# Leaving out the products of zeros at the start of a four-layer transformer kernel

## The chip, the cores and the metric

The kernel runs on one core of one Trainium2 chip. A core has five engines, each working through its own list of instructions in order: TensorE (PE, with its weight loads shown apart as PEld), VectorE (DVE), ScalarE (ACT), GpSimd (POOL) and SyncE (SP), which here only issues DMAs. The metric is the time of one execution on the device in microseconds (us); lower is better.

## The reference

The input x is 2048 tokens of 576 numbers in bf16. Two kinds of layer alternate, A, B, A, B, each added to x after a normalisation of its input:

```python
x = x + A(layernorm(x)); x = x + B(layernorm(x))
x = x + A(layernorm(x)); x = x + B(layernorm(x))

# A: linear attention, 32 heads of 18
q, k, v = split(x @ wqkv)                       # 576 -> 3 * 576
pq = q @ w_phi[h]; pk = k @ w_phi[h]            # per head, 18x18
phi_q = concat(softmax(pq), softmax(-pq)); phi_k likewise
kv = phi_k^T @ v;  z = sum over tokens of phi_k
o = (phi_q @ kv) / (phi_q . z + 1e-6);  return o @ wo
# B: gated, without a nonlinearity
return ((x @ w_gate) * (x @ w_up)) @ w_down     # 576 -> 4608 -> 576
```

## The kernel before

**Stages.** The tokens are cut into 16 tiles of 128. The first microseconds prepare the A layers: `w_phi` and the q and k parts of `wqkv` (loaded as five blocks of rows into `Wraw`) are multiplied together once, so that one product per tile gives pq or pk. For each block this takes five transposes on PE (L1235), a copy out of PSUM (L1238), and products with a block-diagonal form of `w_phi` called `BDphi` (L1249). Then layer A runs over the tiles (projections at L1366, sums at L1608), then layer B in eight pairs of tiles (L1902 for gate and up, L1976 and L1978 for down), and both again for the second pair of layers.

**The flag.** The softmaxes can leave out the subtraction of the maximum when the weights are small enough. The kernel finds out on the chip. `t_flag` forms, for each of the five blocks of `Wraw`, ten products of a 128x128 piece with itself (L1109), summed over the blocks in two PSUM banks; VectorE takes the maxima (L1112), compares them with a bound made from `w_phi` (`t_m2`: L1088 on VectorE, L1091 and L1094 on PE, L1118 on VectorE), two tiny products (L1120) gather the outcome, and VectorE writes the flag (L1122). Every engine then loads the flag (L315) and branches (L316). What follows the branch exists twice, a fast and a general program; all work of the layers lies behind it. Here the fast one runs.

**The order of the work.** The program writes all engines' lists at build time. A planner (`Sched`) holds generators ("threads") that ask for operations, keeps a modelled time for each engine, and takes either the thread that a long list of names written out by hand (`ORDER`) says comes next or, when that list is used up, the one that can start first. A thread that needs a PSUM bank takes the free one whose last modelled use is the oldest (`_try_acquire`, `bank_time`).

**The products of zeros.** `t_init` first has VectorE set a 128x128 tile `zt` to zero (L1005), and then tells the planner that it has a filler (L1007). From there on, whenever the planner is about to place PE work, it calls `keep_warm` with the modelled start of that work. Where PE's modelled gap before it is over 350 ns (1000 ns behind the branch), filler products are put there, each a 128x128 piece of zeros with itself into a free PSUM bank that nothing reads (L1067):

```python
b = max(cand)[1]
cold = 2.0 if t < self.warm_at else 1.0
n = int((limit - (150.0 if early else 400.0) - t) / (56.0 * cold))
for _ in range(n):
    o = self.fill(b, self.pe_mode)
```

They end in the model before the work that they stand in front of. `limit` is the modelled start of that work, `t` is PE's modelled time, `cand` holds the free banks with the time of their last use. In the program that runs there are 25 of them, all ahead of PE's first other instruction.

Of the kernel before, what the change touches and what calls it, by code (L numbers as in the profile page):

```python
# [797 lines left out]
class K:  # L798
# [203 lines left out]
    def t_init(self):  # L1002
        s = self
        yield ("ops", "dve", [
            Op(80, lambda e: e.memset(s.zt[:], 0.0), writes=[("zt",)]),  # L1005
        ])
        s.sc.fill = s.filler  # L1007
        yield ("ops", "dve", [
            Op(100, lambda e: e.memset(s.epst[:], EPS), writes=[("epst",)]),
            Op(100, lambda e: e.memset(s.eps6[:], 1e-6), writes=[("eps6",)]),  # L1010
# [1256 lines left out]
```

## Time and profile before

| | |
|---|---|
| median of 4 runs | 1059.44 us (1058.93 to 1061.63) |
| profiled execution, its own time | 1061.01 us |
| its span, from first to last instruction | 1059.3 us |
| PE busy | 1051.6 us, 99% of the span, 15853 products |
| DVE, ACT, POOL busy | 480.0, 345.6, 193.5 us |
| chain of work that ended last | PE 96%, DMA 2%, DVE 1%, ACT 1% |
| products of zeros (L1067) | 25, from 1.04 us on, the last begun at 3.6 us |
| flag written (L1122) | 11.74 us |

The profile is of one execution. Its busy time of PE counts each product from its start to its modelled end, so neighbours overlap in it; the distance from one start to the next is what a product takes from PE's time. The granted clock is printed as 1.00 in every stretch, the first microseconds too. A releaser behind an idle time is inferred from semaphores. The 1.7 us between span and own time lie before the first and behind the last instruction.

### The profile page before, as it was taken

What the parts mean: (1) busy time and instruction counts of PE and PEld (TensorE: products, weight loads), DVE (VectorE), ACT (ScalarE), POOL (GpSimd) and SP (SyncE); (2) the same over time, 40 slices, a digit from 0 to 9 for tenths busy, and PEclk for the clock granted to TensorE, in tenths of its full rate; (3) what the DMA queues carried; (4) which work ended last, traced back from release to release, by engine and by line L of the source; (5) the groups of instructions that cost most, each with busy time, mean ns of one, the idle gap of its engine ahead of it and who ended that gap; (6) DMA issues with size and microseconds to landing.
All of it is one profiled execution on the core that took longest, in us unless ns stands there. A gap on an engine that the chain in (4) does not pass through costs nothing.

```text
span 1059.3 us, 34388 instructions
## 1 busy us (share of the span) xinstructions
PE 1051.6 (99%) x15853; PEld 804.6 (76%) x15853; DVE 480.0 (45%) x971; ACT 345.6 (33%) x836; POOL 193.5 (18%) x208
## 2 busy tenths in 40 slices
PE   9999999999999999999999999999999999999998
PEld 7778868687786868778696786878777786868684
DVE  7885544354544435444242753534344343424131
ACT  7775314143241414224141732222213131303020
POOL 4952112030222203013010120202010101000000
PEclk9999999999999999999999999999999999999999
DMA  5694281653608164342606035535372818080704
GB/s 172 109 357 134 44 232 38 185 79 92 159 22 229 28 196 68 105 125 42 205 7 202 4 57 166 108 116 135 91 172 57 206 23 239 15 226 15 213 2 149
DMA packets 177626, 127.79 MB, mean 121 GB/s; under 512 B 96576, under 2 KB 175680, under 8 KB 176320
## 3 DMA queue, kind: packets, MB, share of 16 engines
q1 hardware_dynamic: 176864, 125.47, 45.7%
q8 instruction: 126, 2.06, 0.8%
q14 instruction: 28, 0.23, 0.1%
q10 hardware_dynamic: 608, 0.02, 0.0%
HBM read 100.82 MB, written 2.36 MB: 97 GB/s over the span
## 4 chain that ended last, share of the span: by engine, by line
PE 96%; DMA 2%; DVE 1%; ACT 1%; issue 0%
PE ps L1902 54%; PE ps L1976 22%; PE ps L1366 13%; PE ps L1978 3%; PE ps L1760 1%; DMA wdr<-in_B_w_down_dram 1%; PE ps L1608 1%; DMA wdx<-in_B_w_down_dram 0%; PE ps L1354 0%; PE ps L1333 0%; DVE dd_h1g L1569 0%; DMA wst<-in_A_w_phi_dram 0%; PE ps L1249 0%; DVE ss_w4f L1554 0%; ACT dd_h1g L1487 0%; PE ps L1109 0%
## 5 line engine op out<-in xcount | busy, mean ns | idle before, releaser
L1902 PE MATMUL ps<-xT,Wu 64*128 64x256 bf16 x4608 | 581.5, 269 | 0.0
L1902 PE MATMUL ps<-xT,Wg 64*128 64x256 bf16 x4608 | 580.7, 269 | 0.1
L1902 PEld LDWEIGHTS ps<-xT,Wg 64*128 64x128 bf16 x4608 | 430.4, 94 | 31.2 <-issue 3.7
L1902 PEld LDWEIGHTS ps<-xT,Wu 64*128 64x128 bf16 x4608 | 431.6, 94 | 27.8
L1951 DVE TENSOR_TENSOR hT<-ps,hT 128x512 bf16<-128x512 f32 x288 | 199.1, 691 | 302.2 <-ACT hT L1949 302.1
L1949 ACT CAST hT<-ps 128x512 bf16<-128x512 f32 x288 | 168.4, 585 | 401.0 <-PE ps L1902 397.6
L1976 PE MATMUL ps<-wdr,hT 128*128 128x512 bf16 x960 | 245.5, 380 | 0.9 <-DMA wdr<-in_B_w_down_dram 0.8
L1569 POOL TENSOR_TENSOR dd<-dd,ss 128x576 bf16<-128x576 bf16 x92 | 107.1, 1190 | 440.0 <-ACT ss L1565 440.0
L1978 PE MATMUL ps<-wdr,hT 128*128 128x64 bf16 x960 | 184.9, 193 | 0.0
L1976 PEld LDWEIGHTS ps<-wdr,hT 128*128 128x128 bf16 x960 | 93.8, 98 | 112.3 <-DMA wdr<-in_B_w_down_dram 2.9
L1902 PE MATMUL ps<-xT,Wr 64*128 64x256 bf16 x1152 | 164.7, 269 | 0.0
L1322 POOL TENSOR_SCALAR xln<-x_sb,nmean,rstd 128x576 bf16<-128x576 bf16 x58 | 47.2, 822 | 324.9 <-DVE nmean L1303 142.5
L2019 DVE TENSOR_TENSOR x_sb<-ps,x_sb 128x64 bf16<-128x64 f32 x32 | 7.0, 220 | 211.5 <-PE ps L1978 211.5
L1978 PEld LDWEIGHTS ps<-wdr,hT 128*128 128x128 bf16 x960 | 94.1, 98 | 0.2
L1565 ACT ACTIVATE ss<-ss 128x64 f32<-128x64 f32 x92 | 23.8, 260 | 197.9 <-DVE ss L1554 196.9
L1554 DVE TENSOR_REDUCE ss<-dd 128x64 f32<-128x1152 bf16 x48 | 63.7, 1344 | 12.6 <-ACT dd L1487 8.9
L1902 PEld LDWEIGHTS ps<-xT,Wr 64*128 64x128 bf16 x1152 | 62.8, 94 | 6.5
L1976 PE MATMUL ps<-wdx,hT 128*128 128x512 bf16 x192 | 54.3, 380 | 0.2 <-DMA wdx<-in_B_w_down_dram 0.2
L1366 PE MATMUL ps<-Wv,xT 64*128 64x288 bf16 x576 | 49.2, 283 | 0.0
L1366 PE MATMUL ps<-Wk,xT 64*128 64x288 bf16 x576 | 48.0, 283 | 0.3 <-ACT dd_h1g L1487 0.2
L1289 DVE BATCH_NORM_STATS2 st<-x_sb 128x6 f32<-128x288 bf16 x120 | 46.2, 444 | 0.6 <-DMA x_sb<-in_A_x_dram 0.6
L1366 PE MATMUL ps<-Wq,xT 64*128 64x288 bf16 x576 | 41.2, 283 | 0.1
(129 smaller groups left out, 742.8 us busy)
## 6 DMA issues: line engine op xcount, KB each, us to landing
wdr<-in_B_w_down_dram SPq DMA_DIRECT2D x240, 288.0 KB, 3.7
wdx<-in_B_w_down_dram SPq DMA_DIRECT2D x48, 288.0 KB, 3.6
Wg<-in_B_w_gate_dram SPq DMA_DIRECT2D x4, 1152.0 KB, 17.2
Wu<-in_B_w_up_dram SPq DMA_DIRECT2D x4, 1152.0 KB, 18.8
out_dram<-x_sb SPq DMA_DIRECT2D x16, 144.0 KB, 2.4
x_sb<-in_A_x_dram SPq DMA_DIRECT2D x7, 288.0 KB, 3.8
Wraw<-in_A_wqkv_dram SPq DMA_DIRECT2D x5, 304.0 KB, 4.7
xT<-xln SPq DMA_TRANSPOSE x54, 2.5
```

Of the source, the lines that this page charges most:

```text
L1289: ops.append(Op(d_dve(288), (lambda e, j=j, h=h, src=src: e.bn_stats(st[:, sl[j], 6 * h:6 * h + 6], src)), reads=rd, writes=[("st", sl[j], ...
L1322: em = (lambda e, j=j: e.tensor_scalar(xln[:, sl[j], 0:576], x_sb[:, ss[j], :], s.nmean[:, sl[j]:sl[j] + 1], rstd[:, sl[j]:sl[j] + 1], ALU ...
L1366: out.append(Op(61, (lambda e, h=h, k=k, st=(i == 0 and k == 0), sp=(i == 1 and k == 3): e.matmul(s.ps[:, banks[h], 0:N], L[r, k, :], Wm[r ...
L1554: Op(1265, (lambda e: e.tensor_reduce(ss[:, sm, :], e4, AX.X, ALU.add)), reads=s.ddk(sm, 0) + s.ddk(sm, 1), writes=[("ss", sm)]),
L1565: yield ("ops", "act", [Op(200, (lambda e, kw=kw: e.activation(ss[:, sm, :], ss[:, sm, :], **kw)), reads=[("ss", sm)], writes=[("ss", sm)])])
L1569: yield ("alt", [(eng, [Op(dur, (lambda e, ev=ev, rb=rb: e.tensor_tensor(ev, ev, rb, ALU.mult)), reads=s.ddk(sm, br) + [("ss", sm)], write ...
L1608: ops.append(Op(d_pe(CW * n) + 3, (lambda e, k=k, c0=c0, h=h, n=n, st=(first and k == bi): e.matmul(s.ps[:, bank, c0:c0 + CW * n], phi[:, ...
L1902: out.append(Op(54.3, (lambda e, bank=bank, cs=cs, lhsT=lhsT, rhs=rhs, st=st, sp=sp: e.matmul(ps[:, bank, cs].rearrange("p (a n) -> p a n" ...
L1949: yield ("ops", "act", [Op(480, (lambda e, gb=gb, p=p: e.copy(hT[:, p, :], ps[:, gb, :])), reads=[("gu", gb)], writes=[("hT", p)] + (s.raw ...
L1951: yield ("ops", "dve", [Op(600, (lambda e, ub=ub, p=p: e.tensor_tensor(hT[:, p, :], ps[:, ub, :], hT[:, p, :], ALU.mult)), reads=[("gu", u ...
L1976: ops = [Op(d_pe(512), (lambda e: e.matmul(s.ps[:, bank, 0:512], lhsT, s.wslot(slot)[:, fi, 0:512], start=(f == 0), stop=(f == NF - 1))), ...
L1978: Op(d_pe(64) + 3, (lambda e: e.matmul(s.ps[:, z, 64 * sl:64 * sl + 64], lhsT, s.wslot(slot)[:, fi, 512:576], start=(f == 0 and (sl == 0 o ...
```

## The change

The planner is told that it has no filler. `keep_warm` is then never called, and the program has no instruction of L1067. The tile `zt` is still set to zero (L1005), though nothing reads it any more. Nothing else of the text of the kernel differs.

```diff
@@ t_init
             Op(80, lambda e: e.memset(s.zt[:], 0.0), writes=[("zt",)]),
         ])
-        s.sc.fill = s.filler
+        s.sc.fill = None
         yield ("ops", "dve", [
```

## The prediction

> **What bounds the kernel now.** I began with the page: the span and the chain of work that ended last.
>
> ```profile
> span 1059.3 us, 34388 instructions
> ...
> PE 96%; DMA 2%; DVE 1%; ACT 1%; issue 0%
> ```
>
> PE carries 96% of the chain, so what delays PE for good delays the end. But the change touches only the first 4 us, so the question is what bounds that stretch. The tile view of zt tells what goes:
>
> ```profile
> L1067 PE MATMUL ps<-zt x25: 289/314/314, 1.0 to 3.6; 128*128 128x128 bf16 x25
> ```
>
> Then the timeline of PE (start, length, engine, line, operation, operands, count):
>
> ```profile
> 1.04 2.85 PE L1067 MATMUL ps<-zt 128*128 128x128 bf16 x25 [1.04 <-DVE eps L1010]
> 3.87 1.24 PE L1109 MATMUL ps<-Wraw 128*128 128x128 bf16 x10
> 4.91 0.47 PE L1235 MATMUL ps<-ident,Wraw 128*128 128x128 bf16 x5
> 5.22 0.72 PE L1109 MATMUL ps<-Wraw 128*128 128x128 bf16 x10
> 6.09 0.38 PE L1091 MATMUL ps<-identf,cst 128*1 128x128 f32 x2
> 6.40 0.32 PE L1249 MATMUL ps<-BDphi,WTk 128*128 128x144 bf16 x3
> 6.57 0.44 PE L1235 MATMUL ps<-ident,Wraw 128*128 128x128 bf16 x5
> 6.93 0.73 PE L1109 MATMUL ps<-Wraw 128*128 128x128 bf16 x10
> 7.71 0.45 PE L1235 MATMUL ps<-ident,Wraw 128*128 128x128 bf16 x5
> 8.10 0.38 PE L1094 MATMUL ps<-flg,onesf 1*128 1x1 f32 x2
> 8.41 0.73 PE L1109 MATMUL ps<-Wraw 128*128 128x128 bf16 x10
> 8.98 0.31 PE L1249 MATMUL ps<-BDphi,WTk 128*128 128x144 bf16 x3
> 9.13 0.56 PE L1333 MATMUL ps<-ident,xln 128*128 128x128 bf16 x6
> 9.62 0.73 PE L1109 MATMUL ps<-Wraw 128*128 128x128 bf16 x10
> ```
>
> Look at the same ten products of L1109 twice. Those from 3.87 reach to the next line's start at 4.91: 1.04/10, about 104 ns from start to start, and each lasts up to 314 ns. The ten from 5.22, with nothing waiting between them, last 219 ns each and fit into 0.56 us, 56 ns apart. The groups view of each stretch (busy us, mean ns) says the same; first 3.86 to 4.85, then 5.2 to 5.78:
>
> ```profile
> L1109 PE MATMUL ps<-Wraw 128*128 128x128 bf16 x10 | 1.2, 310 | 0.0
> ```
>
> ```profile
> L1109 PE MATMUL ps<-Wraw 128*128 128x128 bf16 x10 | 0.7, 219 | 0.0
> ```
>
> So PE runs at half rate up to about 4.9 us and at full rate from there, although the clock column shows 1.00 throughout. The waits of the weight loads from 3.5 to 12.5 us show how little room PE has in this stretch:
>
> ```profile
> PEld ps L1091 <- DVE cst L1088: 0.3, 1, 0.3
> PEld ps L1109 <- DMA Wraw<-in_A_wqkv_dram: 0.2, 1, 0.2
> PEld ps L1235 <- DMA Wraw<-in_A_wqkv_dram: 0.2, 1, 0.2
> ```
>
> And the chain of work up to 12.6 us (start, length, what) shows where the stretch leads:
>
> ```profile
> 9.69 0.57 PE ps L1109 x8
> 10.26 0.02 issue
> 10.28 0.90 DVE cst L1112 x2
> ```
>
> The last block's products feed the flag with no slack, and every engine branches on it: all four layers lie behind it. Their loads of x, issued at 12.5 us, do too. I see no anchor later that would take a late flag back, so a flag that is d late makes the end d late.
>
> [...]
>
> **The change, part by part.** *Removed:* 25 products of 107 ns, 2.7 us of PE, and as many weight loads beside them. Nobody reads them. The last starts at 3.58 and gives way at 3.69, and the first L1109 begins only at 3.87, since its block issued at 0.79 lands 3.0 us later. So removal itself gains nothing in this execution; where that block lands earlier it gains at most the 0.2 us. A loss from removal itself: none, as nothing waits on them. The zeroing of zt stays, 0.11 us of DVE, with DVE idle until 4.97.
>
> *The order:* the filler took PSUM bank 7, the last of those unused. Without it, the bank's modelled last use is 0 in place of some 3.7 us, and still every used bank has a later one and banks 2 to 6 come first in the list. Products end before the work that they precede, so no modelled start moves. I expect the same instructions in the same order, less 50 on PE. No DMA, wait or queue position moves on SP, ACT, DVE or POOL.
>
> *The rate:* PE's first busy time is now 3.87 and not 1.04. [...] Until then I lay out the same list at half rate: products of 128 columns 107 ns, the three of L1249 0.27 us, the two f32 ones 0.50 for 0.31 (an estimate: twice the streaming, the rest kept), 0.45 for the second pair. Starts, now cold (before): second ten of L1109 5.47 (5.22); L1091 6.54 (6.09); L1249 7.04 (6.40); L1235 7.31 (6.57); third ten 7.84 (6.93); L1235 8.91 (7.71); L1094 9.44 (8.10); fourth ten 9.89 (8.41). The waits of 0.3, 0.2 and 0.2 us above are already swallowed in that. After release the old spacing holds. From the third L1235 to the last ten it is 9.62 - 7.71 = 1.91 us, less at most 0.15 which the last ten perhaps waited for their own block (issued at 4.09, 5.5 us to landing: 9.59).
>
> - Release at 7.3: third L1235 at 7.31 + 0.28 + 0.57 = 8.16, **0.45 late**.
> - At 9.0: 8.91, one product cold, four warm, end 9.24 against 8.00, **1.24 late**.
> - At 10.7: fourth ten end at 10.84 against 8.97, **1.87 late**.
>
> From there the path is fixed: ten products, L1112, L1118, L1120, L1122, branch. PE has a wait of only 0.3 us at L1120, which the chain on DVE pays for, not PE. So d is 0.45 to 1.87, about 1.2. Against this execution: 1061.01 + 1.2 = 1062.2. It had release early (4.9), d = 0. The median stands 1.57 below it[...]. So the median goes to 1059.44 + 1.2 = **1060.6**.
>
> **Rivals.** *Slower by more: the gate stays shut past the branch.* PE's list up to the flag is thinned by transposes (L1235, L1333), 31 of some 100 products. [...] release waits for the dense projections (L1366) behind the branch. The last ten then begin near 12.1, 2.5 late; their products, and the 19 of L1235 and L1249 between them and L1120 take another 2 us at half rate in place of 1.0; the flag is some 3.7 late. The first microseconds of projections at half rate may add up to 3.5. That is +2.2 (released soon after 11 us) to +7: about 1063.1. [...] Against it: once released at 4.9, PE stayed at full rate through just this mix. It decides over 0.2% once release comes later than about 11.3 us.
>
> *Hidden[...].* [...] lateness 0 to 1.2, about 0.4: 1059.8. [...] Against it: the release at 4.9 came after 3.8 us of unbroken products. With luck in the block's landing this case also holds the gain of at most 0.2 us, so 1059.2 at best.
>
> *The change doesn't do what it says:* a different order behind the list written by hand. Only bank 7 could bring it, and by the argument above it doesn't; I count it under the hidden case, with either sign.
>
> **How the numbers follow.** Gate released within 7.3 to 10.7: 0.48, its own range 1059.7 to 1061.4. Shut past the branch: 0.36. Hidden or nothing: 0.16. The bound of what a measurement of this kernel can tell from no change is 0.2%, 2.1 us. The first case lies under it, but the four runs reach 2.2 us above their median, so I give a quarter of it, 0.12, to slower. The second is slower but for 0.02. The third is the same but for 0.05 of luck below. Slower 0.12 + 0.34 = 0.46; same 0.36 + 0.02 + 0.11 = 0.49; faster 0.05. The range runs from 1059.2 to 1064.2, into the middle of the second case and the whole of the third.
>
> **What would show it.** After: no row of L1067; the first L1109 still at about 3.87; products 107 ns apart past 5 us, with the step to 56 ns between 7.3 and 10.7; the flag at 12.2 to 13.6 in place of 11.74, and behind it the same distances as before. Wrong if the flag is later than 14 us[...], if it is on time (PE wasn't the bound), or if the flag is late and the end isn't (a later wait took it back). A changed count of any other line would mean that the order moved.

## The result, and the profile after

The changed kernel takes 1060.51 us in the median of 34 runs (1058.62 to 1062.79), the kernel before 1059.27 in 55 runs (1057.75 to 1062.32). The ratio is 1.0011, with a 95% interval of 1.0006 to 1.0016: slower by 0.6 to 1.7 us, which is clear of no change and lies within the 0.2% named in the prediction. The profiled execution took 1061.62 us of its own time, against 1061.01 before.

First the page: the span, with 50 instructions less, and the chain of work that ended last, whose engine shares are those of before.

```profile
span 1059.8 us, 34338 instructions
...
PE 96%; DMA 2%; DVE 1%; ACT 1%; issue 0%
```

Then the timeline of PE (start, length, engine, line, operation, operands, count, idle time before):

```profile
3.68 1.25 PE L1109 MATMUL ps<-Wraw 128*128 128x128 bf16 x10 [3.68 <-DMA Wraw<-in_A_wqkv_dram]
4.73 0.74 PE L1235 MATMUL ps<-ident,Wraw 128*128 128x128 bf16 x5
5.26 1.27 PE L1109 MATMUL ps<-Wraw 128*128 128x128 bf16 x10
6.46 0.58 PE L1091 MATMUL ps<-identf,cst 128*1 128x128 f32 x2
6.98 0.45 PE L1249 MATMUL ps<-BDphi,WTk 128*128 128x144 bf16 x3
7.26 0.55 PE L1235 MATMUL ps<-ident,Wraw 128*128 128x128 bf16 x5
7.65 0.72 PE L1109 MATMUL ps<-Wraw 128*128 128x128 bf16 x10
8.21 0.44 PE L1235 MATMUL ps<-ident,Wraw 128*128 128x128 bf16 x5
...
10.11 0.73 PE L1109 MATMUL ps<-Wraw 128*128 128x128 bf16 x10
```

No row of L1067 is left. The second ten of L1109 now need 6.46 - 5.26 = 1.20 us to the next row; before they had 56 ns each and were through by 5.8. The five of L1235 at 7.26 are mixed (0.39 us to the next row, where all at half rate would be 0.53 and all at full rate 0.28), and the ten from 7.65 need 0.56. So the full rate begins near 7.5 us, 3.8 us after PE's first work, and no longer near 4.9. Besides what the views print, the traces keep the moments at which the granted clock changed: it became full at 4.96 us before and at 7.53 us after. The last block's ten begin at 10.11 in place of 9.62: 0.49 late.

The chain up to 12.6 us (start, length, what) shows what the lateness displaced. Before, the chain did not lie on PE until 6.09 us, but on the load of `w_phi` and on VectorE's work with it:

```profile
1.31 3.64 DMA wst<-in_A_w_phi_dram
...
4.97 0.91 DVE BDphi L1077
5.88 0.17 DVE cst L1088
...
6.09 0.38 PE ps L1091 x2
```

After, it lies on PE from the first product all the way to the last block's products:

```profile
3.68 1.25 PE ps L1109 x10
4.93 0.53 PE ps L1235 x5
5.47 1.07 PE ps L1109 x10
6.53 0.51 PE ps L1091 x2
7.05 0.39 PE ps L1249 x3
7.43 0.38 PE ps L1235 x5
7.81 0.56 PE ps L1109 x10
8.37 0.28 PE ps L1235 x5
8.65 0.31 PE ps L1094 x2
8.96 0.66 PE ps L1109 x10
9.62 0.14 PE ps L1249 x3
9.77 0.41 PE ps L1333 x6
10.17 0.57 PE ps L1109 x8
```

So PE's slow start first used up the time that PE had spent waiting for VectorE and for blocks of `Wraw`, and only the rest made the flag late.

How far the lateness carries is read from VectorE's timeline. Flag, and one addition of the layers (L1837), before:

```profile
11.74 0.13 DVE L1122 TENSOR_SCALAR flag<-ps 1x1 int32<-1x1 f32 x1
...
119.62 0.45 DVE L1837 TENSOR_TENSOR x_sb<-ps,x_sb 128x288 bf16<-128x288 f32 x1
```

and after:

```profile
12.23 0.14 DVE L1122 TENSOR_SCALAR flag<-ps 1x1 int32<-1x1 f32 x1
...
120.10 0.45 DVE L1837 TENSOR_TENSOR x_sb<-ps,x_sb 128x288 bf16<-128x288 f32 x1
```

0.49 late at the flag, 0.48 at 120 us. (The execution before has the earliest flag of all that were profiled.) Behind that, the two executions part for another reason. The waits of the weight loads for the blocks of w_down (`wdr`, `wdx`), before and then after (us in all, times, longest):

```profile
PEld ps L1976 <- DMA wdr<-in_B_w_down_dram: 2.9, 7, 0.9
PEld ps L1976 <- DMA wdx<-in_B_w_down_dram: 0.5, 1, 0.5
```

```profile
PEld ps L1976 <- DMA wdr<-in_B_w_down_dram: 3.6, 5, 1.3
PEld ps L1976 <- DMA wdx<-in_B_w_down_dram: 1.0, 3, 0.4
```

They fall elsewhere and have other lengths from one execution to the next (in all 3.4 us before, 4.6 after, and 1.5 in one of the runs below). Here they put the last product 1.7 us late (1056.17 against 1054.48), and a shorter tail behind it takes 1.1 back, so that the spans differ by about 0.5. That this is close to 0.48 is chance: spans of single executions can't price a change of this size. The medians of many runs can. The flag of a single trace shows the path, but its moment also moves with the loads, as one of the runs below shows.

### The profile page after: what moved, and what is told of

Same layout as the page of the kernel before. It is cut to its first block, busy times and chain, and to the rows that moved or that the text cites. A ratio compares the mean times of both kernels' runs of the same rounds, so it can differ in the third digit from the quotient of the medians.

```text
span 1059.8 us, 34338 instructions
## 1 busy us (share of the span) xinstructions
PE 1049.6 (99%) x15828; PEld 803.7 (76%) x15828; DVE 480.0 (45%) x971; ACT 345.9 (33%) x836; POOL 193.8 (18%) x208
## 4 chain that ended last, share of the span: by engine, by line
PE 96%; DMA 2%; DVE 1%; ACT 1%; issue 0%
PE ps L1902 54%; PE ps L1976 22%; PE ps L1366 13%; PE ps L1978 3%; PE ps L1760 1%; DMA wdr<-in_B_w_down_dram 1%; PE ps L1608 1%; DMA wdx<-in_B_w_down_dram 1%; PE ps L1354 0%; PE ps L1333 0%; DVE dd_h1g L1569 0%; PE ps L1109 0%; PE ps L1249 0%; DMA Wraw<-in_A_wqkv_dram 0%; DVE ss_w4f L1554 0%; ACT dd_h1g L1487 0%
## 5 line engine op out<-in xcount | busy, mean ns | idle before, releaser
L1554 DVE TENSOR_REDUCE ss<-dd 128x64 f32<-128x1152 bf16 x48 | 63.7, 1344 | 12.6 <-ACT dd L1487 8.9
```

Source lines behind the costliest of these rows:

```text
L1554: Op(1265, (lambda e: e.tensor_reduce(ss[:, sm, :], e4, AX.X, ALU.add)), reads=s.ddk(sm, 0) + s.ddk(sm, 1), writes=[("ss", sm)]),
```

## The experiments

Theory: full rate follows PE's early work (at 4.96 us before, 3.9 us after the first product); without the zeros it comes later (at 7.53), the flag is late by what PE then does at half rate, and the end is as late as the flag. Rivals: the 25 instructions less, the other layout or the program not taken make the difference; or a later wait takes a late flag back. A further question was whether transposes count, that is, bring full rate as products do. The expectations call the moment of full rate the release, or the opening of the gate. Their ranges for it are the author's assumptions, as in the prediction: the trace of before does not show what sets that moment.

**Only the 25.** The change also alters the program behind the branch that is not taken, where the planner had put products of zeros too. This run leaves out the 25 alone.

```diff
-        s.sc.fill = s.filler
+        s.sc.fill = None
...
-        yield ("wait", "branch")
+        yield ("wait", "branch"); s.sc.fill = s.filler
```

> One part of the change alone: the 25 products ahead of PE's first other work are left out, and the planner has its filler back from the branch on, so that the program not taken is that of before. Theory: all of the change's effect, first L1109 at 3.7 to 3.9 us, release 7.1 to 10.7 us, ratio 1.0011 (1.000 to 1.002). Rival that the program not taken, or where instructions lie, makes the difference: ratio 1.000.

Measured: 1.0013 (1.0005 to 1.0022), 1060.78 us against 1059.07. First L1109 at 3.58, full rate near 7.5, flag at 12.14. The whole effect is there.

**Only the other program.** The complement.

```diff
-        yield ("wait", "branch")
+        yield ("wait", "branch"); s.sc.fill = None
```

> The other part of the change alone: the 25 products stay, and from the branch on the planner has no filler, so that the program not taken is that of the changed kernel. Theory (the clock): release at 4.5 to 7.9 us as before, ratio 1.000 (0.9992 to 1.0008). Rival (program size or where instructions lie): ratio about 1.001.

Measured: 0.9997 (0.9989 to 1.0005). The program not taken costs nothing. The profile had a surprise: the flag came at 12.23 although full rate began near 6.6. The timeline of PE:

```profile
7.00 0.44 PE L1235 MATMUL ps<-ident,Wraw 128*128 128x128 bf16 x5
7.41 0.73 PE L1109 MATMUL ps<-Wraw 128*128 128x128 bf16 x10
8.21 0.45 PE L1235 MATMUL ps<-ident,Wraw 128*128 128x128 bf16 x5
```

The ten from 7.41 run at full rate and are done by 7.97, and still the next row starts at 8.21. The chain up to 12.6 us tells why:

```profile
2.66 5.50 DMA Wraw<-in_A_wqkv_dram
8.16 0.05 issue
8.21 0.45 PE ps L1235 x5
```

Its block of `Wraw`, issued at 2.66, took 5.5 us to land here, against 5.0 before. A load that landed 0.5 us later has made this flag 0.49 us late, so a late flag in one trace is put down to the clock only where the chain lies on PE. Yet this span is the shortest of all, 1057.0 us, as PE's weight loads waited only 1.5 us for blocks of w_down, against 3.4 before.

**Zeros of one column.** The same 25 instructions with the same weight loads, but hardly anything streamed. (Here and in the runs below that edit the same line, the products of zeros in the program not taken change too, which by the run above costs nothing.)

```diff
-s.zt[0:rows, :], s.zt[0:rows, :], start=True
+s.zt[0:rows, :], s.zt[0:rows, 0:1], start=True
```

> The kernel before, with the products of zeros 1 column wide instead of 128; their weight loads of 128 columns stay, and so does their number, 25. If the gate counts what the array streams: PE counts as idle until the first ten of L1109 at about 3.7 to 3.9 us, release at 7.1 to 10.7 us, flag 0.4 to 1.9 us late, ratio about 1.001, as in the changed kernel. If any instruction of PE or its weight loads count: release at 4.5 to 7.9 us, ratio 1.000. The rival that it is the instructions less and not the clock: ratio 1.000 with a late release.

Measured: 1.0015 (1.0006 to 1.0024), 1060.19 us. The timeline of PE:

```profile
1.04 0.83 PE L1067 MATMUL ps<-zt 128*128 128x1 bf16 x25 [1.04 <-DVE eps L1010]
3.59 1.25 PE L1109 MATMUL ps<-Wraw 128*128 128x128 bf16 x10 [1.72 <-DMA Wraw<-in_A_wqkv_dram]
...
7.66 1.27 PE L1109 MATMUL ps<-Wraw 128*128 128x128 bf16 x10
8.72 0.68 PE L1235 MATMUL ps<-ident,Wraw 128*128 128x128 bf16 x5
9.33 0.38 PE L1094 MATMUL ps<-flg,onesf 1*128 1x1 f32 x2
9.64 0.73 PE L1109 MATMUL ps<-Wraw 128*128 128x128 bf16 x10
```

The third ten still run at half rate, and full rate begins only near 9.2; the flag came at 12.98, 1.24 late. As many instructions as before, and the loss is there: the count is not the cause. These 25 took only 0.8 us, so this run can't say whether it is their width or their short duration that kept PE at half rate until 9.2.

**Six wide ones.** The other way round: as long a stretch, with 19 instructions fewer.

```diff
-return Op(56, (lambda e: e.matmul(s.ps[:, bank, 0:128], s.zt[0:rows, :], s.zt[0:rows, :], ...
+return Op(224, (lambda e: e.matmul(s.ps[:, bank, 0:512].rearrange('p (a b) -> p a b', a=4), s.zt[0:rows, :],
+    s.zt[0:rows, :].unsqueeze(1).to_broadcast([rows, 4, 128]), ...
```

> The kernel before, with the products of zeros 512 columns wide, 6 of them in place of 25 (6 x 427 ns at half rate, from 1.04 to 3.6 us). Theory that what the array streams opens the gate, however few instructions: release between 4.5 and 7.9 us, flag 0 to 0.7 us late, ratio 1.000 (0.9992 to 1.0008). Rival that the number of PE's instructions makes the difference (19 of the change's 25 are gone here): ratio about 1.001 with an early release.

Measured: 1.0002 (0.9994 to 1.001), 1059.56 us. The timeline of PE:

```profile
1.04 2.74 PE L1067 MATMUL ps<-zt 128*128 128x512 bf16 x6 [1.04 <-DVE eps L1010]
3.59 0.81 PE L1109 MATMUL ps<-Wraw 128*128 128x128 bf16 x10
4.24 0.44 PE L1235 MATMUL ps<-ident,Wraw 128*128 128x128 bf16 x5
4.62 0.73 PE L1109 MATMUL ps<-Wraw 128*128 128x128 bf16 x10
6.44 0.38 PE L1091 MATMUL ps<-identf,cst 128*1 128x128 f32 x2 [1.09 <-DVE cst L1088]
```

Already the first ten of L1109 are through in 0.65 us. Full rate began at about 3.8 us, earlier than the 4.5 expected and 2.7 us after the first of the wide products. The gain on PE then runs into a wait of 1.09 us for VectorE, so it is worth nothing (flag at 11.89). With 19 instructions fewer the time is that of before.

**A flag late by 3 us.** Whether the end follows the flag, with an amount that can be measured.

```diff
-            yield ("ops", "pe", [Op(55, (lambda e, m=m, ...
+            yield ("ops", "pe", [Op(0, (lambda e, bank=banks[0]: e.matmul(s.ps[:, bank, 384:512], s.zt[:], s.zt[:],
+                start=False, ...)), ...)] * (54 if kt == 4 else 0) + [Op(55, (lambda e, m=m, ...
```

> The kernel before, with 54 more products of zeros (128x128, into 128 columns of a PSUM bank that nothing reads) directly ahead of the last ten products of L1109, so that the flag is late by 54 x 56 ns = 3.0 us with the clock at full rate. Theory that a late flag makes the end as late: ratio 1.0028 (+2.8 to +3.0 us). Rival that a later wait takes it back: ratio under 1.0014, and in the trace the distance to before shrinks behind the branch.

Measured: 1.0043 (1.0027 to 1.0058), 1063.80 us in only four runs, 4.7 us up. The expected 1.0028 lies just inside, anything under 1.0014 does not; why the median is above it stays open. VectorE's timeline, to be held against the same two rows above:

```profile
14.82 0.14 DVE L1122 TENSOR_SCALAR flag<-ps 1x1 int32<-1x1 f32 x1
...
122.70 0.45 DVE L1837 TENSOR_TENSOR x_sb<-ps,x_sb 128x288 bf16<-128x288 f32 x1
```

3.08 late at both, and 3.14 at the last product (1057.62). Nothing takes a late flag back up to 122.70 us; the last product's distance also holds waits for w_down that differ from one execution to the next.

**Transposes of zeros.** The 25 as transposes, of which 21 fit.

```diff
-e.matmul(s.ps[:, bank, 0:128], s.zt[0:rows, :], s.zt[0:rows, :], ...)
+e.transpose(s.psb16[bank][:, 0:rows], s.zt[0:rows, :], s.ident[0:rows, 0:rows])
```

> The kernel before, with each of the products of zeros made a transpose of the zeros (moving operand: the identity). 21 of them fit ahead of PE's first other work, from about 1.4 us on (the identity is written at 1.36). Theory ([...] d, the lateness of the flag, follows from the moment of release) with transposes counting as busy: [...] flag 0 to 0.8 us late, ratio to before 1.000 to 1.0003. Theory with transposes not counting[...]: release as without any, 7.1 to 10.7 us, flag 0.4 to 1.9 us late, ratio about 1.001. Rival (it is the 25 instructions less and not the clock): ratio 1.000 whatever the moment of release.

Measured: 1.0002 (0.9994 to 1.001), 1059.17 us, full rate near 6.9, flag at 11.96. The ratio leans to counting, though its interval just reaches the 1.001 of the other reading; the one moment of release, 0.2 us ahead of the 7.1 of that reading, decides nothing. So twice more the same kernel, for the moment alone:

> The kernel with zero transposes in place of the products, once more, for the moment of release alone: the first profile of it had release at 6.9 us, which both theories on transposes allow. [...] A release under 5.5 us settles that they count; one over 7.6 us that they don't.

> The same kernel a third time, for the same reading[...]: release under 5.5 us settles that transposes count as busy, over 7.6 us that they don't.

Full rate began near 7.6 us and near 6.2 us. Neither lies outside the limits of 5.5 and 7.6, which were the author's assumptions, so neither decides. Instead of drawing again, the next run makes the transposes so many that the answer can't be missed.

```diff
-(lambda e: e.transpose(...))
+(lambda e: [e.transpose(...) for _ in range(3)][-1])
```

> Three transposes of zeros in place of each of the 21, so 63 ahead of PE's first other work: at half rate they would last from 1.4 to 8.1 us. If transposes count as busy, the gate opens among them[...] and their distance steps from 107 to 56 ns in midst of the row. If they don't, all 63 stand 107 ns apart, [...] with the first ten of L1109 at half rate from 8.1 us on; the flag would then be over 3 us late.

The tile view of zt up to 20 us (min/median/max ns, first and last start), then the timeline of PE:

```profile
L1067 PE MATMUL ps<-ident,zt x63: 219/314/315, 1.4 to 7.3; 128*128 128x128 bf16 x63
```

```profile
1.41 6.11 PE L1067 MATMUL ps<-ident,zt 128*128 128x128 bf16 x63 [1.41 <-POOL ident L1020]
7.36 0.72 PE L1109 MATMUL ps<-Wraw 128*128 128x128 bf16 x10
```

The row holds both lengths, 314 and 219 ns, and its end at 7.36 is 0.8 us earlier than 63 at half rate would be: full rate began near 6.5, when PE had done nothing but transposes since 1.41. So transposes alone brought full rate, here 5.1 us after the first. Whether they do so as soon as products do is not shown.

## Why the prediction was right

**Removal itself.** Nothing gained, as laid out: in the changed kernel the first L1109 waited for its block, which landed 0.2 us earlier than in the execution before. Its start differs by as much from one execution to the next (3.58 to 3.93 us, without the run of 63 transposes).

**The order.** Right for the program that runs: the same instructions less the 50, row for row. For the program not taken it was wrong to say nothing of it: its order does move, as its products of zeros go too. It costs nothing (0.9997 alone).

**The rate.** Release between 7.3 and 10.7 was expected; seen were 7.5 (after), 7.5 (only the 25) and 9.2 (one column). But the range, and with it the three moments at which the prediction lays out its list, was the author's assumption, and what sets the moment is not shown by the runs either. It is no fixed time after PE's first work. The trace of before and that of only the other program begin with the same 25 products at 1.04 us, and full rate came at 4.96 in the one and near 6.6 in the other, 3.9 and 5.6 us later. With six wide products it came 2.7 us after the first of them (1.04 to 3.8), without zeros 3.8 and 3.9 us after the first L1109 (3.68 to 7.5 and 3.58 to 7.5), and with one column 5.6 us after it (3.59 to 9.2).

**The size.** The median moved 1.24 us and 1.2 was predicted; that they agree so closely is luck. The 1.2 belongs to a release at 9.0, which was assumed. In the two profiles without the 25, release was near 7.5 and the last ten were 0.40 and 0.49 late, where the prediction's own list gives 0.45 at 7.3. Nor does a start with the 25 always bring release as early as in the execution that the prediction counts from (4.9): in the run of only the other program it came near 6.6. The interval of the medians is 0.6 to 1.7; the runs can't tell a mean lateness of 0.7 from one of 1.2. Nor does the outcome by itself say much, as no change beyond 0.2% had been given 0.49 and slower 0.46; what held is the path.

**The late flag by the moment of release.** The prediction's list held where the chain lies on PE. Release read from the step in the spacing, lateness of the last ten against 9.62:

| kernel | full rate from about | last ten | late |
|---|---|---|---|
| six wide | 3.8 | 9.77 | 0.15 |
| before | 4.9 | 9.62 | 0 |
| zero transposes, third | 6.2 | 9.71 | 0.09 |
| only the other program | 6.6 | 10.11 | 0.49 |
| zero transposes | 6.9 | 9.84 | 0.22 |
| only the 25 | 7.5 | 10.02 | 0.40 |
| after | 7.5 | 10.11 | 0.49 |
| zero transposes, again | 7.6 | 10.23 | 0.61 |
| one column | 9.2 | 10.86 | 1.24 |

Two rows fall out of the order for the reasons shown above: six wide waited for VectorE, only the other program for its block of `Wraw`. Expected were 0.45 at 7.3 and 1.24 at 9.0, less up to 0.15.

**Late flag, late end.** Right, shown with 3.08 us carried to 122.70 us unchanged, and by a median that is 2.9 us later even at the low end of its interval.

**The gate shut past the branch** did not happen in any profile: the latest full rate, with one column, began near 9.2 us, and that flag came at 12.98. The doubt was whether transposes bring full rate; the 63 transposes brought it alone, near 6.5 us. The prediction gave this rival 0.36, too much; the trace of before, where PE's step (4.96) came as its first transposes began (4.91 us), could not have told.

**Hidden** fell too: an interval from 1.0006 excludes no effect and, with 0.6 us at its low end, the 0.4 that this case gave as its middle. In the profiles without the zeros, or with zeros of one column, full rate came at 7.5 us or later.

No run beat the kernel before clearly: with the other program's fillers gone (0.9997) or with six wide products (1.0002) it is the same.

## What to carry to other kernels

What a late TensorE clock costs is worth laying out instruction by instruction: take the list of PE's work ahead of the first point that everything waits for, double the distance of starts up to the release (here 107 ns in place of 56 for products of 128 columns; the two f32 ones took 0.52 us in place of 0.31), and let existing waits swallow what they can. Here PE's first work came 2.6 us later, and the median 1.2 us. For an effect this small, take the size from the median over many runs, and from the trace the path: the lateness at the branch, and whether the chain ahead of it lies on PE or on a load. The span of a single profile also holds other waits, here those for w_down: 3.4 us before, 4.6 after and 1.5 in only the other program.

## What the runs showed of the hardware that was not expected

- Transposes alone brought TensorE to full rate: with 63 of zeros and nothing else, the distance of starts stepped from 107 to 56 ns at about 6.5 us, 5.1 us after the first.
- Full rate came as early as 2.7 us after the first product in one execution, with products of 512 columns (1.04 to 3.8 us).
- The moment of full rate moves from execution to execution: 6.2, 6.9 and 7.6 us in three of the same kernel. In the traces of before and after, the change of the granted clock to full and the one back to half, behind the last product, lie 1054.72 and 1051.31 us apart.
- Zeros of one column, 25 with full weight loads, passed in 0.83 us from the first start to the last end, in an execution at half rate up to about 9.2 us.
- The clock column of the profile showed 1.00 through the stretch at half rate in every run; in the views, only the spacing and the lengths of the products show it.
